# Linear attention and a squared-ReLU layer on one core: the carried product in 64x64 tiles read from the compact state, and a new order of all operations

## Chip, cores and metric

The kernel runs on one core of a Trainium2 chip. The time is device microseconds of one execution; three runs of the kernel before took 183.14, 184.62 and 185.03 us. The engines are TensorE (PE in the profile, with its weight loads as PEld), VectorE (DVE), ScalarE (ACT), GpSimd (POOL) and SyncE (SP), whose queue issues all DMAs here.

## The reference

```python
def _attn_ref(r, k, v, w, u):           # (4, 8, 768, 48) each, u (8, 48)
    for t in range(S):
        cur = einsum('bhd,bhe->bhde', u[None] * kt, vt)
        y[:, :, t] = einsum('bhd,bhde->bhe', rt, state + cur)
        state = wt[:, :, :, None] * state + einsum('bhd,bhe->bhde', kt, vt)
...
    x = attn_out.transpose(0, 2, 1, 3).reshape(B * S, H * D)     # 3072 x 384
    g = maximum(x @ w_in, 0) ** 2                                # 3072 x 2048
    return g @ w_out                                             # 3072 x 384
```

A linear attention with a decay per channel runs over 768 positions for 4 batches of 8 heads of width 48. Its output is the input of a two-layer network with a squared ReLU between the layers.

## The kernel before, in words

**Tiling.** The 768 positions of a batch are cut into three steps of 256 positions, so there are 12 steps s = 0 to 11. Each step has two chunks c = 0, 1 of 128 positions, and a row of a tile holds two neighbouring positions j = 0, 1. The eight heads are treated as four pairs; `e` is the head in a pair. In a chunk, the attention is a masked product within the chunk, and a product of r with the state that is carried over from earlier chunks.

**The operations of a step**, by the names that the order uses (line of the kernel before, engine):

- `ld.s.x` loads w, r, k, v of a step (L168, 384 KB each) on SP; `ld.g.i` and `ld.g.o` load quarters of the two weights (L178, L184), which `cast` makes bf16 (L190, on ACT, DVE or POOL).
- `ww_` multiplies neighbouring decays (L248), `lw_` takes the logarithm (L252, ACT), `cum_` sums it with three kinds of products (L309 to L312, TensorE): two triangular sums and the sum of a chunk. `exp_` (L317) and `ac_` (L322) are exponentials on ACT.
- `rw_`, `kw_` (L273, L277) multiply r and k with decays; `rd_.s.1` and `rd_.s.0` (L335, L332, DVE) make the decayed k and r. They are transposed by TensorE (`tr_`, L346, with copies `rkt_`, L359 and L362) in steps 0 to 3, or by a DMA transpose (`dtr_`, L369, L371) later.
- `p_` (L385, TensorE, 64x64 tiles) makes the scores, `pm_` (L395, L398, DVE) masks them, `y_` (L441) multiplies them with v.
- `ku_`, `qp_`, `q_`, `qs_`, `vq_` (L284, L289, L293, L264, L302) make the term of u and of the position itself; `v_` and `vs_` (L259, L264) are casts of v.
- `su_` (L412, TensorE, 64x64 tiles with 48 columns) makes what a chunk adds to the state, `ts_` (L420, L422) adds it to the state, and `sn_` (L427, POOL) multiplies by the chunk's decay and writes the state S as bf16, 128 rows (two heads of 64) by 4 pairs by 48 columns. This is the compact form.
- `sb_` (L436) copies S into a block-diagonal buffer of 128 rows by 4 pairs by 2 x 48 columns, one copy for each half of the rows, the other half staying zero from four clears at the start (L234, POOL).
- `yc_` (L441 too) is the carried product: for each chunk four products, one for each pair, of full 128x128 weights (r transposed) with 96 columns of that buffer. It adds into the same bank as `y_`.
- `ysb_` (L463, DVE) adds the u term and evicts y, `yt_` and `xt_` (L472, L477) or the DMA transpose `dyt_` transpose it to xT.
- `m1_.s.g` (L492, 8 groups of 6 products), `rl_` (L501 on ACT, L503 on DVE), `sq_` (L509, L511), `m2_.s.c.q` (L517, 8 pieces of 4 products), `os_` (L524, L526) and `store` (L530) are the two-layer network.
- `warm_.n.b` (L534) issues n filler products into bank b; nothing reads them.

**What sets the order.** One string, ORDER, lists every operation. The program records them in that order, and each engine runs its own operations strictly in the order of the list, SP's DMAs too. A suffix `=A`, `=V`, `=G` picks ACT, DVE or POOL, and `:0`, `:1`, `:m`, `:b` pick the PSUM bank. PSUM holds two double banks `att`, two banks `bk` and two banks `m`.

The carried product, its buffer and the list's start:

```python
    def sb_(s, c):
        t = tiles["S", s + c, 1 - c]
        b = tiles["sb", s + c, 1 - c] = sb_bufs[(2 * s + c - s // NB) % NSB]
        for e in range(2):
            rows = slice(e * DP, (e + 1) * DP)
            copy_on("sb_", s, c)(b[rows, :, e, :], t[rows])
...
ld.0.w ww_.0=V ld.0.k kw_.0=G lw_.0 warm_.9.0 cum_.0:0 exp_.0 rd_.0.1 warm_.8.1 tr_.0.1:0 rkt_.0.1=A ld.0.r
```

Of the kernel before, what the change touches and what calls it, by code (L numbers as in the profile page):

```python
# [22 lines left out]
rkt_.1.1=V vs_.1.0=A v_.1=A warm_.1.2 tr_.1.0:1 ysb_.0=V lw_.2 rkt_.1.0=V warm_.4.2 yt_.0:0 sn_.0.1 sb_.0.1=A
ac_.1 vs_.1.1=G q_.1 qs_.1=G p_.1.1:0 p_.1.0:m vq_.1=G cast.i.2=A cast.i.1=A xt_.0=V pm_.1.0 su_.1:b ts_.1.0=V
cum_.2:1 sn_.1.0 pm_.1.1 cast.i.0=G m1_.0.4:0 m1_.0.5:1 sb_.1.0=A y_.1:0 yc_.1 ts_.1.1=V rl_.0.5=V ysb_.1=V
rl_.0.4=A m1_.0.2:1 rl_.0.2=A ld.2.k m1_.0.3:0 ld.2.r kw_.2=G rl_.0.3=A exp_.2 ld.3.i yt_.1:0 sn_.1.1
m1_.0.0:1 m1_.0.1:0 cast.i.3=G ld.2.v ku_.2=V xt_.1=V rl_.0.0=A ac_.2 rl_.0.1=A m1_.1.0:1 qp_.2=G rw_.2=V
# [5 lines left out]
y_.2:1 yc_.2 m2_.0.0.1 rl_.1.7=A sq_.0.3=A m2_.0.1.2 m2_.0.0.2 m2_.0.1.3 m2_.0.0.3 ww_.3=V lw_.3 ld.3.v
os_.0.1=A os_.0.0=A cum_.3:0 ysb_.2=V yt_.2:1 xt_.2=V exp_.3 ac_.3 rl_.1.5=V sq_.1.3=A sq_.1.2=A m2_.1.0.0:0
m1_.2.3:1 ld.4.w vs_.3.0=G kw_.3=V qp_.3=V m1_.2.1:0 m2_.1.0.1 rw_.3=G rl_.2.1=A v_.3=A rl_.2.3=A m2_.1.0.2
m2_.1.0.3 ww_.4=G m1_.2.5:0 rd_.3.1 su_.3:1 ld.4.r ld.4.k q_.3 vs_.3.1=A rd_.3.0 m1_.2.4:1 os_.1.0=A qs_.3=G
ts_.3.0=A sn_.3.0 rl_.2.4=V tr_.3.1:1 lw_.4 kw_.4=G tr_.3.0:0 rw_.4=G rkt_.3.1=A cum_.4:0 exp_.4 rl_.2.5=V
m1_.2.0:1 ld.4.v rl_.2.0=A m1_.2.2:0 m2_.1.1.0:1 rl_.2.2=A m2_.1.1.1 ts_.3.1=V rkt_.3.0=V sn_.3.1 rd_.4.1
ku_.4=G vq_.3=G p_.3.0:m v_.4=A ac_.4 sq_.2.2=A sb_.3.0=A rd_.4.0 pm_.3.0 ld.6.w su_.4:1 p_.3.1:0 m2_.1.1.2
m2_.1.1.3 ld.5.k pm_.3.1 m1_.2.6:0 y_.3:0 yc_.3 qp_.4=G sq_.2.1=A sq_.2.0=A m1_.2.7:1 ld.5.w os_.1.1=V  # L40
m2_.2.0.0:0 ts_.4.0=V dtr_.4.1 dtr_.4.0 sb_.3.1=A rl_.2.6=A sn_.4.0 ld.6.v ld.6.k ld.5.r ww_.5=G ysb_.3=V q_.4
yt_.3:1 m2_.2.0.1 ts_.4.1=V m2_.2.0.2 p_.4.1:0 p_.4.0:1 rl_.2.7=V sq_.2.3=V xt_.3=A m2_.2.1.0:1 vs_.4.1=A
lw_.5 m1_.3.2:0 store.1.0 m1_.3.3:1 qs_.4=G pm_.4.1 sn_.4.1 rl_.3.2=A vs_.4.0=G cum_.5:0 m1_.3.0:0 rl_.3.3=A
vq_.4=G sb_.4.0=V pm_.4.0 ac_.5 ww_.6=G m1_.3.7:1 exp_.5 m2_.2.0.3 sq_.3.1=A y_.4:1 rl_.3.0=V rl_.3.7=A yc_.4
ld.6.r rw_.6=G m1_.3.1:0 ku_.5=G qp_.5=G m1_.3.4:1 ld.7.w store.1.1 os_.2.0=A ku_.6=G m2_.2.1.1 kw_.5=V
rw_.5=V kw_.6=V rl_.3.1=A lw_.6 m1_.3.5:0 ld.5.v ysb_.4=V store.2.0 cum_.6:1 ww_.7=G ld.8.w yt_.4:0 ld.7.k
kw_.7=G rd_.5.1 rd_.5.0 xt_.4=V rl_.3.4=A sq_.3.0=A rl_.3.5=A exp_.6 m1_.3.6:1 v_.6=A m2_.2.1.2 rl_.3.6=V
m2_.3.0.0:0 m1_.4.3:0 v_.5=A m2_.2.1.3 ac_.6 su_.5:0 rd_.6.1 rd_.6.0 rl_.4.3=V dtr_.5.0 su_.6:1 ts_.5.0=V
sq_.3.2=A sb_.4.1=A dtr_.5.1 q_.5 sq_.3.3=A os_.2.1=A vs_.5.0=A lw_.7 dtr_.6.0 qs_.5=A vs_.5.1=A ld.7.v ld.7.r
m1_.4.7:1 m1_.4.5:0 rl_.4.5=V m2_.3.0.1 m2_.3.0.2 m2_.3.0.3 m1_.4.6:0 ts_.6.0=V sn_.6.0 sn_.5.0 sb_.5.0=A  # L50
ts_.6.1=V qp_.6=G vs_.6.0=G p_.5.1:0 p_.5.0:1 rl_.4.7=V m2_.3.1.0:1 m1_.4.0:1 rl_.4.6=V pm_.5.1 dtr_.6.1
sq_.4.3=A os_.3.0=A vq_.5=G m2_.3.1.1 rl_.4.0=V pm_.5.0 vs_.6.1=A cum_.7:0 m2_.3.1.2 m1_.4.1:0 y_.5:1 ac_.7
# [535 lines left out]
```

## Time and profile before

| | us |
|---|---|
| median of three runs | 184.62 |
| the profiled execution, its own time | 184.86 |
| its span | 182.9 |
| TensorE busy | 173.3 |
| DVE busy | 141.3 |
| ACT busy | 131.9 |
| POOL busy | 114.4 |
| first m1_ product starts | 23.70 |

The span runs from the first to the last instruction that the profiler shows; the execution's own time is 2.0 us more. A row of the groups by form reads: line, engine, operation, tiles, shape and count, then busy time and mean ns of one, then the engine's idle time before these instructions and what ended it. A row of the chain of waits in order of time reads: start, length, what; a row of the timeline likewise with the engine first. TensorE's products overlap in the pipe, so the mean of one product in a group row is longer than the spacing of its starts, and the price of a stretch is read from the starts of what follows.

### The profile page before, as it was taken

The numbers are of one execution on the slowest core, as the hardware profiler recorded it, in microseconds if no ns is written. First come the engines' busy times: TensorE is split into PE (matmuls) and PEld (weight loads), VectorE is DVE, ScalarE is ACT, GpSimd is POOL, SyncE is SP. The second block draws the span as 40 slices with busy tenths as digits, with TensorE's granted clock in tenths as the row PEclk, the third lists the DMA queues.
The fourth block names the chain that finished last, engine by engine and source line by source line (L and its number), as shares of the span: only waits on it lengthen the run. The fifth ranks groups of instructions, "written<-read, shape, count | busy, mean of one in ns | idle before, by whom it ended". The sixth has DMA issues, their size and how long they took to land.

```text
span 182.9 us, 5277 instructions
## 1 busy us (share of the span) xinstructions
PE 173.3 (95%) x2150; PEld 124.2 (68%) x2150; DVE 141.3 (77%) x218; ACT 131.9 (72%) x237; POOL 114.4 (63%) x151
## 2 busy tenths in 40 slices
...
GB/s 141 267 268 303 380 287 345 373 286 236 224 271 142 230 291 292 147 159 199 264 203 167 272 191 189 192 193 282 144 109 87 117 47 88 72 61 86 0 128 90
DMA packets 79208, 35.80 MB, mean 196 GB/s; under 512 B 72400, under 2 KB 77648, under 8 KB 79184
## 3 DMA queue, kind: packets, MB, share of 16 engines
...
q8 instruction: 17, 0.28, 0.7%
...
## 4 chain that ended last, share of the span: by engine, by line
PE 69%; DVE 8%; ACT 8%; DMA 7%; issue 5%; POOL 1%; DVEq 0%; ACTq 0%; POOLq 0%
PE m L492 28%; PE bk L517 27%; DMA xT<-y_sb 5%; PE att L441 4%; PE bk L534 3%; ACT gt L501 2%; PE att L385 2%; DMA w_raw<-in_w_dram 2%; DVE rdec_buf L332 2%; ACT att L317 2%; DVE gt L503 1%; ACT v_bf L259 1%; DVE y_sb L463 1%; ACT gt L509 1%; POOL ku L302 1%
## 5 line engine op out<-in xcount | busy, mean ns | idle before, releaser
L492 PE MATMUL m<-xT,wi_sb 128*128 128x256 bf16 x576 | 73.9, 273 | 1.3 <-DMA xT<-y_sb 1.0
L517 PE MATMUL bk<-wo_sb,gt 128*128 128x384 bf16 x384 | 71.8, 326 | 0.0
L492 PEld LDWEIGHTS <-wi_sb 128*128 128x128 bf16 x576 | 55.0, 98 | 14.4 <-DMA xT<-y_sb 1.8
L501 ACT ACTIVATE gt<-m 128x512 f16<-128x512 f32 x60 | 35.4, 595 | 22.9 <-PE m L492 22.1
L517 PEld LDWEIGHTS <-gt 128*128 128x128 bf16 x384 | 36.7, 98 | 19.4 <-ACT gt L509 0.2
L509 ACT ACTIVATE gt<-gt 128x1024 bf16<-128x1024 f16 x37 | 38.4, 1053 | 4.1 <-DVE gt L503 3.8
L503 DVE TENSOR_SCALAR gt<-m 128x512 f16<-128x512 f32 x36 | 24.6, 687 | 10.6 <-PE m L492 10.3
L398 DVE TENSOR_TENSOR pmT<-att,mask 128x1024 bf16<-128x1024 f32 x19 | 22.8, 1216 | 0.1
L284 POOL TENSOR_TENSOR ku<-k_raw,u_bc 128x768 f32<-128x768 f32 x10 | 18.5, 1854 | 5.0 <-DMA k_raw<-in_k_dram 5.0
L302 POOL TENSOR_TENSOR ku<-v_sh,qs 128x768 f32<-128x768 bf16 x11 | 16.3, 1479 | 1.9 <-ACT qs L264 1.4
L289 POOL TENSOR_TENSOR ku<-ku,r_raw 128x768 f32<-128x768 f32 x9 | 16.7, 1850 | 0.2
L427 POOL TENSOR_TENSOR S<-t_state,ac_buf 128x192 bf16<-128x192 f32 x20 | 11.7, 588 | 4.1 <-DVE t_state L420 1.8
L264 POOL COPY qs<-q 64x8 f32<-64x8 f32 x32 | 6.3, 196 | 12.8 <-DVE q L293 11.7
L335 DVE TENSOR_TENSOR kdec_buf<-k_raw,att 128x768 bf16<-128x768 f32 x12 | 11.4, 948 | 3.7 <-ACT att L317 2.5
L332 DVE TENSOR_TENSOR rdec_buf<-r_raw,att 128x384 bf16<-128x384 f32 x24 | 12.2, 548 | 1.3 <-ACT ac_buf L322 1.1
L534 PE MATMUL bk<-warm 128*128 128x512 bf16 x33 | 11.9, 510 | 1.2 <-DVE half_ones L220 1.2
L264 POOL CAST v_sh<-v_raw 64x384 bf16<-64x384 f32 x20 | 10.7, 535 | 3.2 <-DMA v_raw<-in_v_dram 2.3
L463 DVE TENSOR_TENSOR y_sb<-att,ku 128x768 bf16<-128x768 f32 x12 | 11.4, 953 | 1.5 <-PE att L441 0.7
L436 ACT COPY sb_buf<-S 64x192 bf16<-64x192 bf16 x32 | 11.1, 346 | 2.0 <-POOL S L427 1.8
L524 ACT ACTIVATE o_sb<-bk 128x384 f32<-128x384 f32 x12 | 5.8, 487 | 8.7 <-PE bk L517 8.1
L277 POOL TENSOR_TENSOR k_raw<-k_raw,w_raw 128x384 f32<-128x384 f32 x8 | 8.7, 1082 | 5.2 <-DMA k_raw<-in_k_dram 5.2
L511 DVE TENSOR_TENSOR gt<-gt 128x1024 bf16<-128x1024 f16 x11 | 7.8, 715 | 5.3 <-ACT gt L501 5.1
...
## 6 DMA issues: line engine op xcount, KB each, us to landing
...
rT<-rdec_buf SPq DMA_TRANSPOSE x16, 3.5
```

What stands on the lines that cost most here:

```text
L264: copy(out[j * Q:(j + 1) * Q, c], src[c * Q:(c + 1) * Q, :, j])
L284: tensor_mul("ku_", s)(ku[:], raw["k", s][:, :, 1:3, :], u_bc[:, :, None, :].to_broadcast([C, H, 2, D]))
L289: tensor_mul("qp_", s)(ku[:], ku[:], raw["r", s][:, :, 0:2, :])
L302: tensor_mul("vq_", s)(vq[:], tiles["vs", s][:], tiles.pop(("qs", s))[:, :, :, None].to_broadcast([C, 2, H, D]))
L332: nc.vector.tensor_mul(rdec[0][:, :, j, :, 0:D], x[:, :, j, :].rearrange("p (a e) d -> p a e d", e=2), dec.rearrange("p (a e) d -> p a e d ...
L398: nc.vector.tensor_mul(pmT, ps_p[:].rearrange("p e (x t) -> p (e x) t", x=4), mk.to_broadcast([C, 8, C]))
L492: nc.tensor.matmul(ps1[:, j, :], wi_sb[:, n // 4, kk, n % 4 * 128:(n % 4 + 1) * 128], tiles["xT", s][:, :, kk, :], start=(kk == 0), stop=( ...
L501: nc.scalar.activation(rl, m1, AF.Relu, scale=RS)
L503: nc.vector.tensor_scalar(out=rl, in0=m1, scalar1=RS, scalar2=0.0, op0=ALU.mult, op1=ALU.max)
L509: nc.scalar.activation(gt, rl, AF.Square)
L517: nc.tensor.matmul(m2, gt[:, n, c * C:(c + 1) * C], wo_sb[:, n, :], start=(n == 0), stop=(n == NT - 1))
L534: nc.tensor.matmul((bk + m1_bank)[i][:] if i < 4 else att[i - 4][:, 0, :], warm[:, 0:C], warm[:], start=True, stop=True)
```

## The change

- `sb_`, its four buffers and their clears are gone. `yc_` takes a chunk, and makes 16 products for it, one for each pair, position j and head e, of 64x64 weights with 48 columns read from S itself; four of them lie in the four quarters of the array. The list holds 20 such `yc_`, where 12 stood, and places each by itself.
- y lies in its double bank by head e, and no longer by chunk, so `ysb_` reads it in runs of 48. S has six buffers in place of four.
- All operations can take half of the heads, a chunk of a step, or further banks, and there is an operation `al_` that would make the second decay sum on DVE. The list uses no half and no `al_`: both sums stay on TensorE.
- The list is new throughout. By engine, of the operations that changed their place (before, then after): `rw_` POOL 8, 12; `kw_` POOL 8, 10; `ww_` POOL 8, 10; `ku_` POOL 10, 12; `qp_` POOL 9, 11; `qs_` ACT 4, 7; `vs_` DVE 3, 0 and ACT 11, 14; `v_` POOL 4, 2 and ACT 8, 10; `sq_` ACT 37, 41 and DVE 11, 7; `rl_` ACT 60, 59; `os_` ACT 12, 14; casts of the weights on ACT 3, 5, on DVE 2, 0, on POOL 3, 3; `rkt_` ACT 3, 4; filler products 42, 39. TensorE transposes as before in steps 0 to 3, and for y in steps 0 to 5.

```diff
-ld.0.w ww_.0=V ld.0.k kw_.0=G lw_.0 warm_.9.0 cum_.0:0 exp_.0 rd_.0.1 warm_.8.1 tr_.0.1:0 rkt_.0.1=A ld.0.r
-rw_.0=V ld.1.w ww_.1=G rd_.0.0 warm_.4.2 tr_.0.0:1 ld.0.u ku_.0=V qp_.0=V q_.0 ac_.0 lw_.1 ld.1.k ld.0.v
-ld.1.r ld.1.v warm_.1.0 cum_.1:1 rkt_.0.0=A warm_.1.0 p_.0.0:m kw_.1=G ld.2.w pm_.0.0 p_.0.1:0 pm_.0.1 ku_.1=G
...
+ld.0.w ww_.0=V lw_.0 warm_.11.0 cum_.0:0 ld.0.k kw_.0=V exp_.0 rd_.0.1 warm_.8.1 tr_.0.1:0 rkt_.0.1=A ld.0.r
+rw_.0=G rd_.0.0 ld.0.u ld.1.w warm_.3.2 tr_.0.0:1 rkt_.0.0=A ac_.0 ld.0.v ld.1.k ld.1.r ku_.0=G ld.1.v ld.1.i
+warm_.5.2 p_.0.0:1 ww_.1=V qp_.0=V lw_.1 cum_.1:0 ld.0.i v_.0=A su_.0:m ts_.0.0=A pm_.0.0 p_.0.1:1 ld.2.w
+kw_.1=V exp_.1 vs_.0.0=G q_.0 sn_.0.0 vs_.0.1=A rd_.1.1 ld.3.i ld.2.i pm_.0.1 ac_.1 warm_.7.1 tr_.1.1:0
+vs_.1.1=A rkt_.1.1=A rw_.1=G qs_.0=G rd_.1.0 vq_.0=G warm_.2.1 y_.0:1 yc_.0.1:1 tr_.1.0:1 vs_.1.0=A ku_.1=G
+ysb_.0=V ld.2.k cast.i.1=A warm_.1.4 yt_.0:0 rkt_.1.0=V ts_.0.1=V xt_.0=V v_.1=G ld.2.r p_.1.1:0 p_.1.0:m
+pm_.1.0 pm_.1.1 su_.1:b sn_.0.1 yc_.1.0:1 m1_.0.3:0 qp_.1=G cast.i.0=A ld.2.v m1_.0.2:1 rl_.0.3=A ww_.2=G
+warm_.1.4 m1_.0.1:0 q_.1 lw_.2 rl_.0.2=A qs_.1=G ts_.1.0=V sn_.1.0 y_.1:1 warm_.1.4 m1_.0.0:1 cum_.2:0 vq_.1=G
+ld.0.o cast.i.3=A yc_.1.1:1 sq_.0.1=A rl_.0.1=V m1_.0.7:0 ts_.1.1=V rl_.0.0=V cast.i.2=G ld.1.o m1_.0.6:1
+ysb_.1=V rl_.0.7=A yt_.1:0 rl_.0.6=A ld.2.o m1_.0.5:0 exp_.2 rl_.0.5=A sn_.1.1 m1_.0.4:1 xt_.1=V ld.3.o
...
-    NSB = 4
-    sb_bufs = [consts.tile([C, HP, 2, D], BF16, name=f"sb_buf{i}") for i in range(NSB)]
...
-        for t in sb_bufs:
-            nc.gpsimd.memset(t[:], 0.0)
...
-    def sb_(s, c):
...
-    def yc_(s):
-        for c in range(0 if s % NB else 1, 2):
-            for p in range(HP):
-                y_mm(s, c, slice(2 * p * D, (2 * p + 2) * D),
-                     tiles["rT", s][:, c, 2 * p:2 * p + 2, :].rearrange("p j t -> p (j t)"),
-                     tiles["sb", s, c][:, p].rearrange("p e d -> p (e d)"))
+    def yc_(s, c):
+        rT, S_c = tiles["rT", s], tiles["S", s, c]
+        for p in range(HP):
+            for j in range(2):
+                for e in range(2):
+                    y, fresh = y_bank(s, e, slice(j * Q, (j + 1) * Q))
+                    rows = slice(e * DP, (e + 1) * DP)
+                    nc.tensor.matmul(y[:, c, p, :], rT[rows, c, 2 * p + j, :], S_c[rows, p, :],
+                                     start=fresh, stop=True, skip_group_check=True)
...
+        nc.vector.tensor_add(
+            tiles["ysb", s][:, x].rearrange("p c (a e d) -> p (c a) e d", e=2, d=D),
+            tiles["y", s][:, :, cols].rearrange("p e (x d) -> p x e d", d=D),
+            tiles["vq", s][:, x].rearrange("p c (a e) d -> p (c a) e d", e=2))
```

More of the change, by code (lines that the diff above doesn't have):

```diff
@@ L23 @@
[L23 to L27, printed above, removed]
@@ L33 @@
[L33 to L37, printed above, removed]
@@ L38 @@
[L38 to L52, printed above, removed]
@@ new lines @@
+m2_.4.1.0:0 ld.8.r pm_.6.1 exp_.7 rw_.7=G ww_.8=G yt_.5:1 xt_.5=A store.3.0 rd_.7.0 m2_.4.1.1 kw_.7=G sn_.6.1
+ku_.7=G lw_.8 m1_.4.5:0 rl_.4.5=A qs_.6=A m1_.5.0:1 sq_.4.2=A store.2.1 rl_.5.0=V m2_.4.0.0:1 m1_.5.3:0
+vq_.6=G ac_.7 m2_.4.0.1 y_.6:0 dtr_.7.0 rl_.5.3=V rd_.7.1 m1_.5.5:1 qp_.7=G m1_.5.2:0 v_.7=A yc_.6.1:0 su_.7:1
+ysb_.6=V rl_.5.5=A dyt_.6 vs_.7.1=A rl_.5.2=A dtr_.7.1 m1_.5.7:1 m2_.4.0.2 ts_.7.0=V rl_.5.7=A sn_.7.0
+m1_.5.6:0 cum_.8:0 sq_.5.1=A rl_.5.6=V kw_.8=G rw_.8=G exp_.8 m1_.5.4:1 rl_.5.4=A q_.7 m1_.5.1:0 rl_.5.1=V
```

353 lines of the change are left out of this document (200 added, 153 removed).

## The prediction

> **What bounds the kernel now.** I read the table of engines first, then the chain of waits in order of time, then the groups by form, then TensorE's timeline.
>
> ```profile
> PE 173.3 (95%) x2150; PEld 124.2 (68%) x2150; DVE 141.3 (77%) x218; ACT 131.9 (72%) x237; POOL 114.4 (63%) x151
> ```
>
> TensorE is busy 95% of a span of 182.9 us. Whether that is work or waiting is read from the chain, which gives the price of each kind of TensorE work in a dense stretch (start, length, what):
>
> ```profile
> 29.70 1.45 PE m L492 x12
> 31.99 0.89 PE bk L346 x16
> 49.89 0.37 PE att L412 x32
> 58.72 0.59 PE att L441 x20
> 62.25 0.58 PE att L385 x32
> 62.83 0.76 PE bk L517 x4
> 67.28 0.74 PE att L441 x24
> 87.08 0.36 PE att L385 x16
> 127.16 1.31 PE m L492 x12
> 128.47 1.30 PE bk L517 x8
> 174.37 5.21 PE bk L517 x32
> ```
>
> The reader is to see unit prices. A first-layer group m1_ (6 products) costs 1.31/2 = 0.655 us, a second-layer piece m2_ (4) 1.30/2 = 0.65. Transposes cost 0.89/16 = 0.056 each. The rows of 20 and 24 differ by four carried products, so one chunk of yc_ costs 0.15 us and y_ 0.44. From 29.70 on, where the seventh m1_ group starts, TensorE still has 90 m1_ (59.0 us), 96 m2_ (62.4) and the attention of ten steps: y_ and yc_ 10 x 0.74 less three half ones 0.45 (6.95), 9 cum_ at 0.43 (3.9, timeline rows below), p_ and su_ 9.7 (prices below), 4 yt_ and 4 tr_ (56 transposes, 3.1). That is 145.0 us of work. The last product ends at 174.37 + 5.21 = 179.6, so 3.3 us are tail. 182.9 - 29.7 - 145.0 - 3.3 = 4.9 us are stalls. So the kernel is 29.7 us of opening and then TensorE's own work, with little to win between.
>
> ```profile
> 44.17 0.24 PE L309 MATMUL att<-half_ones,lw_buf 128*128 128x2 bf16 x4
> 44.60 0.50 PE L472 MATMUL bk<-ident,y_sb 128*128 128x128 bf16 x6
> ```
>
> **Part 1, the carried product.** The old form is 80 full-array products; the new one is 320 products of 64x64 with 48 columns (20 chunks of 16), the shape of su_ at L412 (64x64, 48 columns). The p_ rows of 16 and 32 give what a run of small tiles costs: the second 16 add 0.58 - 0.36 = 0.22, so 0.14 us is entry; and four m2_ products after a run take 0.76 instead of 0.65, so 0.11 us is exit. A run costs 0.25 us beside its work. su_ then has 0.37 - 0.14 = 0.23 for 32, so 16 cost 0.115, and a chunk of yc_ that stands next to other small tiles is 0.035 us cheaper than today's 0.15, while one that stands alone costs 0.365. In the two orders I count 17 runs of small tiles before and 24 after; from the seventh m1_ group on, 14 and 19. Of the 20 chunks, 17 come after that point. Sum: 5 x 0.25 - 17 x 0.035 = +0.7 us on TensorE. (p_ and su_ above: 14 x 0.25 + 10 x 0.67 less four half su_ 0.46 = 9.7.) Bounds: 0 if all hides behind stalls; if the small products ran at p_'s 0.22 us per 16, 17 x 0.07 + 1.25 = +2.4. I take 0.7, from the same shape.
>
> [...]
>
> **Part 2, the copies of the state go.** sb_ leaves ACT and DVE, four clears leave POOL, and yc_ waits for sn_ directly, so the state is there two copies (2 x 0.346 = 0.7 us) earlier. Where it is late all the same, whatever stands behind that yc_ in TensorE's list waits with it. The eviction ysb_ now reads its bank in runs of 48; L463 takes 0.953 and two L332 pieces of 384, which read so, 1.10, so it costs DVE 0 to 12 x 0.14 = 1.8 us, off the path. I take 0.
>
> ```profile
> L436 ACT COPY sb_buf<-S 64x192 bf16<-64x192 bf16 x32 | 11.1, 346 | 2.0 <-POOL S L427 1.8
> L436 DVE COPY sb_buf<-S 64x192 bf16<-64x192 bf16 x8 | 2.3, 290 | 0.1
> L264 DVE CAST v_sh<-v_raw 64x384 bf16<-64x384 f32 x6 | 3.4, 564 | 0.1
> L284 POOL TENSOR_TENSOR ku<-k_raw,u_bc 128x768 f32<-128x768 f32 x10 | 18.5, 1854 | 5.0 <-DMA k_raw<-in_k_dram 5.0
> L289 POOL TENSOR_TENSOR ku<-ku,r_raw 128x768 f32<-128x768 f32 x9 | 16.7, 1850 | 0.2
> L302 POOL TENSOR_TENSOR ku<-v_sh,qs 128x768 f32<-128x768 bf16 x11 | 16.3, 1479 | 1.9 <-ACT qs L264 1.4
> L427 POOL TENSOR_TENSOR S<-t_state,ac_buf 128x192 bf16<-128x192 f32 x20 | 11.7, 588 | 4.1 <-DVE t_state L420 1.8 <-DVE t_state L422 1.0 <-ACT t_state L420 0.8
> L264 POOL COPY qs<-q 64x8 f32<-64x8 f32 x32 | 6.3, 196 | 12.8 <-DVE q L293 11.7
> L273 POOL TENSOR_TENSOR r_raw<-r_raw,w_raw 128x384 f32<-128x384 f32 x8 | 8.0, 999 | 1.9 <-DMA r_raw<-in_r_dram 1.8
> ```
>
> **Part 3, the new order's split.** POOL gains two ku_ and two qp_ (4 x 1.85 = 7.4 us), four rw_, two kw_, two ww_ (8 x 1.0 = 8.0), and loses 12 of the small qs copies (2.4) and a few casts and clears: about +10, to 124. ACT gives up 11.1 of sb_ and takes four squares, casts and qs copies for about as much. DVE sheds at least 2.3 + 3.4 of the rows above and four rw_, four squares, two ku_: some 15 to 20 us. All this lies beside TensorE in part 1's terms, as long as no engine's list becomes longer than TensorE's. Before, DVE and ACT are that full; after, POOL and ACT are. I therefore keep the 4.9 us of stalls (bounds 1.5 and 10, in the rivals).
>
> **Part 4, the opening.** The filler products at the start become 11 instead of 9, ww_.0's load, k's multiply (now DVE) and cum_.0 keep their times.
>
> ```profile
> 1.19 4.02 PE L534 MATMUL bk<-warm 128*128 128x512 bf16 x9 [1.19 <-DVE half_ones L220]
> 5.93 0.26 PE L309 MATMUL att<-half_ones,lw_buf 128*128 128x2 bf16 x4 [0.72 <-ACT lw_buf L252]
> 6.65 3.62 PE L534 MATMUL bk<-warm 128*128 128x512 bf16 x8
> 7.78 0.95 DVE L335 TENSOR_TENSOR kdec_buf<-k_raw,att 128x768 bf16<-128x768 f32 x1 [2.52 <-ACT att L317]
> 10.06 0.76 PE L346 MATMUL bk<-ident,kdec_buf 128*128 128x128 bf16 x8
> 10.65 1.03 PE L534 MATMUL m<-warm 128*128 128x512 bf16 x4
> ```
>
> Eight fillers from 6.65 hold TensorE until 10.06, 0.43 us each; the four at 10.65 take about 0.22 each. The first transposes wait for those slow fillers, since their input is ready at 8.75 (7.78 + 0.95, the row of L335). TensorE came to full speed about 4 us after the 0.72 us gap at 5.2 to 5.9, though it had worked 4.0 us before the gap. Eleven fillers end at about 6.0 and close that gap. I take it that full speed comes by about 7, and the transposes start at 8.9. Bounds: 10.2 (no change, and 0.1 us later through the two more fillers) and 8.8. [...]
>
> ```profile
> L362 ACT COPY kT<-bk 128x1024 bf16<-128x1024 bf16 x2 | 2.0, 1004 | 3.2 <-PE bk L346 3.2
> L252 ACT ACTIVATE lw_buf<-ww 128x384 bf16<-128x384 f32 x12 | 6.2, 519 | 3.0 <-DVE ww L248 2.9
> L259 ACT CAST v_bf<-v_raw 128x768 bf16<-128x768 f32 x8 | 6.5, 832 | 0.0
> L317 ACT ACTIVATE att<-att 128x768 f32<-128x768 f32 x12 | 9.6, 802 | 1.1 <-PE att L312 1.0
> L332 DVE TENSOR_TENSOR rdec_buf<-r_raw,att 128x384 bf16<-128x384 f32 x24 | 12.2, 548 | 1.3 <-ACT ac_buf L322 1.1
> L398 DVE TENSOR_TENSOR pmT<-att,mask 128x1024 bf16<-128x1024 f32 x19 | 22.8, 1216 | 0.1
> L395 DVE TENSOR_TENSOR pmT<-m,mask 128x512 bf16<-128x512 f32 x10 | 6.4, 685 | 2.2 <-PE m L385 2.2
> L463 DVE TENSOR_TENSOR y_sb<-att,ku 128x768 bf16<-128x768 f32 x12 | 11.4, 953 | 1.5 <-PE att L441 0.7 <-issue 0.6 <-POOL ku L289 0.2
> L293 DVE TENSOR_REDUCE q<-ku 128x16 f32<-128x768 f32 x12 | 11.4, 946 | 0.6 <-POOL ku L289 0.5
> L477 DVE COPY xT<-bk 128x768 bf16<-128x768 bf16 x5 | 2.8, 553 | 2.3 <-PE bk L472 2.3
> L190 POOL CAST wi_sb<-w_st 128x1536 bf16<-128x1536 f32 x2 | 2.9, 1464 | 1.1 <-DMA w_st<-in_moe_w_in_dram 1.1
> ```
>
> From 8.9 I walk the new order with these means. ACT: from 9.6 two copies (2.0), ac_ and lw_ (0.7), v_.0 (0.83), su_.0 with its copy (0.7), exp_.1 (0.80) = 14.7. DVE is at q_.0 until 14.95 and then runs without a gap: rd_.1.1 0.95, pm_.0.1 1.22, rd_.1.0 1.10, ysb_.0 0.95, copy 0.7, ts_ 0.35, xt_.0 0.55, pm_.1.0 1.37, pm_.1.1 1.22, q_.1 0.95 = 24.3 (the 0.7 and 0.35 are estimates by size from L477). xt_.0 ends at 20.8 and the first m1_ follows su_.1 and yc_.1.0 at about 21.5. POOL then does qs_ 0.78, sn_ 0.59, vq_ 1.48 and the last cast of the first weights 1.46, so the seventh m1_ starts at 24.3 + 4.3 = 28.6, where before had it at 29.7: -1.1 us, with the same work behind it. Without the early full speed all slides by some 1.2 us and the gain is gone (29.8). The loads: on SP's queue k of step 3 is now the fourth load behind the second weights and not the second. Its first reader waited 5.0 us at L284 before. Now three multiplies (ww_.3, rw_.3, ww_.4, 3.0 us) stand ahead of that reader on POOL, and I price the later landing at 0; bounds 0 to 3.
>
> **The sum.** The profiled execution took 184.86 us, 0.24 over the median of 184.62 and inside 183.14 to 185.03. 184.86 - 1.1 (opening) + 0.7 (carried product) + 0 (stalls, tail: the last pieces keep their sequence of square, m2_, os_ and store) = 184.5 us. Likeliest case's own range: 183.0 to 186.3.
>
> **The rivals.** About 1% (1.85 us) is what can be told from no change.
> *TensorE stays slow at the start:* the seventh m1_ at 29.8: 184.5 + 1.2 = 185.7. For it: one gap is thin evidence.
> *DVE's relief pays:* the chain before runs over DVE's rd_, rl_ and ysb_ at several places; with 15 to 20 us less on DVE, stalls fall from 4.9 to about 1.5: 184.5 - 3.4 = 181.1. Against: ACT stays as full.
> *POOL becomes the bound (slower):* summed over the order from the first m1_ to y_.10, POOL has 113 us of work and TensorE 117. By 28.6 some 5 and 6 us of these are done. POOL's 108 then end at 136.6, TensorE's 111 at 139.6, so the old 4.9 us of stalls cover 139.6 + 4.9 - 136.6 = 7.9 us of waits on POOL. Its rows above show 5.0, 12.8, 4.1, 1.9, 1.9 us of waits. If 12 us of these remain, TensorE waits 12 - 7.9 = 4.1 us more: 188.6. It decides from 7.9 us on. Against: q, on which the largest hangs, comes from a DVE with more room.
> [...]
>
> **How the numbers follow.** Forecast 0.32, slow start 0.08, DVE's relief 0.28, POOL 0.27, 25 ns 0.05. Faster by over 1% (below 182.8): 0.28. Within 1%: 0.32 + 0.08 = 0.40. Slower (above 186.5): 0.27 + 0.05 = 0.32. The range, 181.0 to 189.0, takes in the relief at 181.1 and POOL's 188.6, and leaves out about 2 in 10, the tails beyond them.
>
> **What would show it.** Right: 16 yc_ products in about 0.12 to 0.37 us by their neighbours; fillers at 0.22 us from about 7 on and the first transposes near 8.9; first m1_ near 21.5, seventh near 28.6; POOL above 65% with TensorE's stalls still near 5 us. Wrong: POOL's waits for q or loads followed by TensorE waiting for rd_ or y_sb; a first transpose after 10; a yc_ chunk above 0.4 us.

## The result and the profile after

The changed kernel took 186.62 us (median; 185.55 to 188.41) against 184.22 for the kernel before on the same chip: ratio 1.0104, interval 1.0054 to 1.0153. It is slower by about 2 us, where 184.5 and a small gain were forecast.

The profiled execution of the changed kernel had a disturbed clock (0.83 of full speed from 100 to 110 us, against 1.00 elsewhere), so after 29 us, unless the text says otherwise, the rows come from e2, a copy with one word of the list moved at about 95 us (below; 186.49 us, clock 1.00 throughout).

The engines of the changed kernel:

```profile
PE 172.6 (92%) x2387; PEld 123.6 (66%) x2387; DVE 122.7 (66%) x183; ACT 136.3 (73%) x233; POOL 120.4 (65%) x145
```

DVE lost 18.6 us, POOL gained 6.0 and ACT 4.4. TensorE's share fell from 95% to 92%: what was added is waiting. Its opening (timeline: start, length, engine, what):

```profile
1.19 4.00 PE L577 MATMUL bk<-warm 128*128 128x512 bf16 x11 [1.19 <-DVE half_ones L227]
5.78 0.25 PE L323 MATMUL att<-half_ones,lw_buf 128*128 128x2 bf16 x4 [0.59 <-ACT lw_buf L267]
6.21 1.89 PE L577 MATMUL bk<-warm 128*128 128x512 bf16 x8
8.25 0.62 PE L373 MATMUL bk<-ident,kdec_buf 128*128 128x128 bf16 x8
21.56 1.48 PE L535 MATMUL m<-xT,wi_sb 128*128 128x256 bf16 x12
29.03 2.98 PE L535 MATMUL m<-xT,wi_sb 128*128 128x256 bf16 x24 [0.31 <-ACT gt L544]
```

The fillers run at 0.24 us each from 6.2 on, the first transposes start at 8.25 (10.06 before), the first m1_ at 21.56. Eleven fillers took 4.00 us where nine took 4.02 (0.36 us each against 0.45), so some of them ran near the 0.24 us of the later ones already, and a gap of 0.59 us was still left behind them. e2 starts the seventh m1_ group at 28.43, 1.25 us ahead of before. The carried product in e2's chain of waits:

```profile
68.18 0.37 PE att L492 x32
68.55 0.76 PE bk L560 x4
85.30 0.12 PE att L492 x16
93.97 0.24 PE att L492 x16
```

A chunk of 16 costs 0.12 us beside other small tiles and 0.24 by itself, two cost 0.37, and the full-array work after a run takes the 0.11 us more. So neither the opening nor the product went against the forecast. Where the time went is read from two stretches, up to the seventh m1_ and from there to the end (length, then busy time of TensorE as the first engine). The kernel before, then e2:

```profile
29.68:182.90 153.22, 147.28 (x1838) 109.43 (x1837) 117.90 (x179) 110.89 (x197) 93.27 (x113) 1.00 0.84 180
```

```profile
28.43:184.70 156.27, 147.25 (x2042) 109.11 (x2042) 101.55 (x148) 116.17 (x203) 100.46 (x108) 1.00 0.81 179
```

TensorE is as busy as before (147.3 us), but idle for 9.0 us and not 5.9; 3.3 us of both lie in the tail after 145 us. The stretch is 3.05 us longer, and that less the lead of 1.25 is the span's growth of 1.8. By stages, before and e2:

```profile
30.00:50.00 20.00, 19.90 (x246) 14.99 (x246) 17.82 (x28) 18.08 (x32) 11.98 (x13) 1.00 1.02 290
50.00:84.00 34.00, 32.56 (x490) 24.36 (x479) 28.79 (x46) 30.68 (x60) 29.15 (x35) 1.00 1.10 220
84.00:104.00 20.00, 19.39 (x296) 14.83 (x294) 18.18 (x28) 16.19 (x33) 18.01 (x23) 1.00 1.16 215
104.00:145.00 41.00, 40.54 (x540) 30.48 (x536) 34.80 (x53) 29.57 (x49) 31.86 (x39) 1.00 0.94 177
```

```profile
30.00:50.00 20.00, 18.38 (x232) 13.37 (x231) 14.28 (x22) 15.49 (x22) 16.94 (x19) 1.00 1.06 297
50.00:84.00 34.00, 33.89 (x536) 25.61 (x536) 28.45 (x44) 30.97 (x58) 30.48 (x33) 1.00 0.97 195
84.00:104.00 20.00, 17.67 (x299) 13.40 (x298) 13.67 (x22) 17.72 (x36) 16.86 (x18) 1.00 1.05 226
104.00:145.00 41.00, 39.36 (x629) 29.36 (x629) 29.78 (x41) 31.93 (x59) 32.67 (x37) 1.00 1.04 201
```

Idle in the four stages: 0.10, 1.44, 0.61 and 0.46 us before; 1.62, 0.11, 2.33 and 1.64 in e2. The new list waits from 30 to 50 us, from 84 to 104 and later, and saves 1.3 us between. What these waits are (e2, timelines of ACT and TensorE):

```profile
41.07 1.47 ACT L199 CAST wo_sb<-w_st 128x1536 bf16<-128x1536 f32 x1 [0.85 <-DMA w_st<-in_moe_w_out_dram]
49.42 0.18 ACT L345 ACTIVATE ac_buf<-att 128x8 f32<-128x8 f32 x1 [1.74 <-DVE rdec_buf L357]
```

```profile
42.59 2.85 PE L560 MATMUL bk<-wo_sb,gt 128*128 128x384 bf16 x16 [0.31 <-ACT wo_sb L199]
50.06 0.25 PE L323 MATMUL att<-half_ones,lw_buf 128*128 128x2 bf16 x4 [1.25 <-ACT lw_buf L267]
103.26 0.65 PE L419 MATMUL att<-rT,kT 64*64 64x128 bf16 x32 [1.74 <-DMA kT<-kdec_buf]
```

At 41 us ACT waits for the last quarter of the second weights, and m2_ waits for the cast. At 50 us the sum of step 4 waits for its logarithm, which stands behind `ac_.3`. At 103 us the scores of step 7 wait for a transpose, and at 84.87 they wait 0.60 us for another.

### The profile page after: what moved, and what is told of

The parts are those of the page before. It is cut to its first block, busy times and chain, and to the rows that moved or that the text cites. A ratio compares the mean times of both kernels' runs of the same rounds, so it can differ in the third digit from the quotient of the medians.

```text
span 186.6 us, 5700 instructions
## 1 busy us (share of the span) xinstructions
PE 172.6 (92%) x2387; PEld 123.6 (66%) x2387; DVE 122.7 (66%) x183; ACT 136.3 (73%) x233; POOL 120.4 (65%) x145
## 2 busy tenths in 40 slices
DMA packets 79208, 35.81 MB, mean 192 GB/s; under 512 B 72400, under 2 KB 77648, under 8 KB 79184
## 4 chain that ended last, share of the span: by engine, by line
PE 54%; DMA 4%; DVE 4%; POOL 3%; SPq 3%; ACT 2%; issue 2%; ACTq 0%; POOLq 0%; DVEq 0%
PE bk L560 23%; PE m L535 22%; SPq L400 3%; DMA kT<-kdec_buf 2%; DMA xT<-y_sb 2%; PE att L482 2%; PE att L419 2%; PE att L492 1%; DVE rdec_buf L357 1%; POOL ku L296 1%; POOL ku L315 1%; PE att L325 1%; DVE pmT L430 1%; PE att L445 1%; DVE pmT L433 1%
## 5 line engine op out<-in xcount | busy, mean ns | idle before, releaser
L552 ACT ACTIVATE gt<-gt 128x1024 bf16<-128x1024 f16 x41 | 42.5, 1055 | 1.0 <-DVE gt L546 0.6
L296 POOL TENSOR_TENSOR ku<-k_raw,u_bc 128x768 f32<-128x768 f32 x12 | 21.9, 1825 | 0.3 <-DMA u_bc<-in_u_dram 0.3
L301 POOL TENSOR_TENSOR ku<-ku,r_raw 128x768 f32<-128x768 f32 x11 | 20.0, 1821 | 0.2
L460 POOL TENSOR_TENSOR S<-t_state,ac_buf 128x192 bf16<-128x192 f32 x20 | 10.3, 514 | 12.6 <-DVE t_state L455 10.8
L276 ACT CAST v_sh<-v_raw 64x384 bf16<-64x384 f32 x28 | 14.2, 508 | 4.8 <-PE att L482 3.8
L285 POOL TENSOR_TENSOR r_raw<-r_raw,w_raw 128x384 f32<-128x384 f32 x12 | 12.1, 1005 | 5.4 <-DMA r_raw<-in_r_dram 5.3
L306 DVE TENSOR_REDUCE q<-ku 128x16 f32<-128x768 f32 x12 | 11.3, 946 | 1.9 <-POOL ku L301 1.8
L263 POOL TENSOR_TENSOR ww<-w_raw 128x384 f32<-128x384 f32 x10 | 10.4, 1042 | 3.0 <-DMA w_raw<-in_w_dram 3.0
L569 DVE TENSOR_SCALAR o_sb<-bk 128x384 f32<-128x384 f32 x10 | 5.5, 555 | 9.0 <-PE bk L560 9.0
L339 ACT ACTIVATE att<-att 128x768 f32<-128x768 f32 x12 | 9.6, 801 | 2.4 <-PE att L327 2.4
```

What stands on the lines that cost most here:

```text
L276: copy(out[j * Q:(j + 1) * Q, c], src[c * Q:(c + 1) * Q, :, j])
L285: tensor_mul("rw_", s, h)(raw["r", s][:, hs, 2, :], raw["r", s][:, hs, 1, :], raw["w", s][:, hs, 0, :])
L296: tensor_mul("ku_", s, h)(tiles["ku", s][:, hs], raw["k", s][:, hs, 1:3, :], u_bc[:, hs, None, :].to_broadcast([C, n, 2, D]))
L301: tensor_mul("qp_", s, h)(ku, ku, raw["r", s][:, heads(h), 0:2, :])
L552: nc.scalar.activation(gt, rl, AF.Square)
```

## The experiments

Theory A: the new list leaves too little room for DMA: loads and SyncE's queue run in absolute time, take the opening's lead back, and make TensorE wait. Theory B: the list's own order of words does it, whatever the loads do. The rival from the prediction: the small products themselves cost the time. The expectations use more letters: Q and L stand for theory A, O for the list's wait at 50 us (part of B), M for the small products and P for POOL as the bound. All ratios are to the kernel before on the same chip. Edits of the list are shown by the words that move, with a word or two around them, and not by whole lines.

### e1: the changed kernel again

No edit.

> The changed kernel as it is, for an undisturbed profile and a tighter ratio. Theory Q (the new order's DMA list delays loads and transposes, so TensorE's stalls grow from 4.9 to about 7 us): ratio 1.010 to 1.013, span near 184.8, TensorE idle at the same four places (cum_.4, the kT transpose of step 6, xT of step 6, step 9 to 10). Theory M (small tiles cost more than the 0.7 us that I gave them): the same time, but the rows of yc_ cost over 0.4 us a chunk and the idle places vary. Theory P (POOL is the bound): TensorE's idle times end with POOL's work.

Measured: 186.87 us, 1.0109 (1.0070 to 1.0147). The slowdown repeats.

### e2: step 6's transpose ahead of step 7's

```diff
 y_.6:0
-dtr_.7.0
...
 dyt_.6
+dtr_.7.0
```

> One word of the order moved: the transposes of r of step 7 go to the queue behind the transpose of y of step 6. Theory Q: xT of step 6 lands some 2.5 us earlier, TensorE's 2.0 us of idle before the first product of step 6 shrinks to under 0.5, and the time falls by 1 to 2 us against the changed kernel (ratio to before 1.000 to 1.005). Theories M and P: no change beyond 0.3 us.

Measured: 186.49 us, 1.0102 (1.0069 to 1.0134). The changed kernel's own wait near 102 us:

```profile
102.06 1.74 PE L535 MATMUL m<-xT,wi_sb 128*128 128x256 bf16 x12 [1.96 <-DMA xT<-y_sb]
```

It is gone in e2, but the next product that needs a DMA transpose waits 1.74 us at 103.26 (above). Changing places in a late queue moves the wait.

### e3: the changed kernel with nine fillers

```diff
-lw_.0 warm_.11.0 cum_.0:0
+lw_.0 warm_.9.0 cum_.0:0
```

> The changed kernel with 9 filler products at the start in place of 11, so the gap before the first decay sum is open again. My step on the opening: TensorE stays slow until about 10, the first transposes start at 10.1 in place of 8.3, the first m1_ at about 22.7 in place of 21.6, and the time grows by 1.0 to 1.5 us. If the opening is hidden behind loads, the seventh m1_ stays at 29.0 and the time is the same.

Measured: 186.68 us, 1.0110 (1.0061 to 1.0159): the same time without the early start. Its timelines of TensorE and ACT:

```profile
22.41 1.49 PE L535 MATMUL m<-xT,wi_sb 128*128 128x256 bf16 x12
50.13 0.25 PE L323 MATMUL att<-half_ones,lw_buf 128*128 128x2 bf16 x4 [1.25 <-ACT lw_buf L267]
```

```profile
40.62 1.47 ACT L199 CAST wo_sb<-w_st 128x1536 bf16<-128x1536 f32 x1 [0.19 <-DMA w_st<-in_moe_w_out_dram]
```

The first m1_ starts 0.99 us later than in e2 (21.42), yet cum_.4 only 0.07 later. The last weights come at 40.6 here and at 41.1 in e2, so whoever is early waits for them: m2_ starts at 42.66 and 42.59. In these two traces the lead of the opening has ended behind this load. One pair of traces is thin evidence, though: with the same list and the same loads up to there, cum_.4 starts at 50.06 in e2, 49.70 in e15 and 49.30 in e13, and of e3's other executions it is not known whether they started as late (the last section has nine fillers with an early start).

### e4 and e8: the new product in the old order

e4 takes the new operations in the list of before, without `sb_`; e8 then moves the first chunk of the eight two-chunk steps away from the second.

```diff
-y_.4:1 rl_.3.0=V rl_.3.7=A yc_.4
+y_.4:1 rl_.3.0=V rl_.3.7=A yc_.4.0 yc_.4.1
```

```diff
-y_.4:1 rl_.3.0=V rl_.3.7=A yc_.4.0 yc_.4.1
+yc_.4.0:1 y_.4:1 rl_.3.0=V rl_.3.7=A yc_.4.1
```

> The order of before with the new carried product alone: no copies of the state, and each yc_ replaced in place by its one or two chunks of small products. By my prices a run of small tiles of its own costs 0.25 us, 12 of them 3.0 us, and 20 chunks save 0.7: +2.3 us on TensorE, less what the missing copies free on ACT (11 us of work) and DVE (2 us). Theory Q: +0.5 to +2.3 us, ratio 1.003 to 1.012. Theory M: +4 us or more. If the copies' waits were what held before up: faster, ratio below 0.997.

> The kernel with the product alone, and in the eight steps that have two chunks the first chunk moved ahead of y_, so that one more run of small tiles stands alone in each: eight runs more at 0.25 us, +2.0 us against the product alone (ratio to before 1.015 + 0.011 = 1.026) if entering and leaving the small tiles is what costs. If the product alone is slow for another reason (a wait on the state, the eviction's new reading): within 0.6 us of it, ratio 1.013 to 1.018.

Measured: e4 187.7 us, 1.0154 (1.0108 to 1.0200); e8 189.03 us, 1.0250 (1.0210 to 1.0290). Before has 17 runs of small tiles, e4 29, e8 37. By the prices of the prediction e4 should cost 12 x 0.25 less 20 x 0.035, so 2.3 us; the ratio gives 2.8. e8 should cost 8 x 0.25 = 2.0 more; the ratios give 1.8. TensorE's busy time from the seventh m1_ on is 147.28 us before, 149.14 in e4 and 150.36 in e8, so about two thirds of the cost are its own work; the rest is waits. That e8 has the same products as e4 and only more runs shows what this work is: entering and leaving small tiles. The new list, which puts the chunks beside `p_` and `su_`, has 24 runs.

### e5: the full-array product in the new order

```diff
-            for j in range(2):
-                for e in range(2):
...
-                    nc.tensor.matmul(y[:, c, p, :], rT[rows, c, 2 * p + j, :], S_c[rows, p, :],
...
+            e, a = p % 2, p // 2 * 2
+            y, fresh = y_bank(s, e, slice(0, C))
+            nc.tensor.matmul(y[:, c, a:a + 2, :], rT[:, c, 2 * p:2 * p + 2, :].rearrange("p j t -> p (j t)"),
+                             S_c[:, a:a + 2, :].rearrange("p a d -> p (a d)"), start=fresh, stop=True, skip_group_check=True)
```

> The changed kernel with the carried product in the old shape: four full-array products of 96 columns for each chunk, at the same places of the list and after the same waits, reading the compact state as if it were the block-diagonal one; the values of the carried part are therefore not the reference's, and no copies are made. By the prices of the rows (a run of small tiles 0.25 us, 24 runs become 14, a chunk 0.15 in place of 0.115) TensorE has 1.8 us less work. If the small tiles explain what the change lost after 50 us: 1.2 to 2.0 us faster than the changed kernel, ratio to before about 1.000 to 1.004. If the shape costs nothing and the new order alone is slower: ratio stays at 1.009 to 1.012.

Measured: 187.75 us, 1.0187 (1.0147 to 1.0226). The expectation's count of 14 runs was a mistake: the chunks stand between small tiles, so taking them out leaves 22. By the prices it should have come out within 0.2 us of the changed kernel; it is some 1 us slower, and TensorE is busier, not more idle (from the seventh m1_ on; e2 had 147.25):

```profile
28.66:185.70 157.04, 148.01 (x1838) 110.33 (x1838) 101.18 (x148) 115.72 (x202) 100.53 (x108) 1.00 0.84 178
```

So in this order the small products do not cost time; they save 0.8 us of busy time. Why 0.8 and not 0.1 is not settled.

### e6: step 4's logarithm ahead of step 3's exponentials

```diff
+lw_.4
 exp_.3 rd_.3.0 ac_.3
-lw_.4
```

> The changed kernel with one word moved: the logarithm of step 4 stands ahead of the exponential of step 3 on ScalarE, so it no longer waits behind ac_.3, which waits for rd_.3.0. Theory O (the opening's lead is lost at this wait): cum_.4 starts at 48.8 in place of 50.1, TensorE's idle 1.25 us ahead of it goes, and the time falls by 0.8 to 1.3 us against the changed kernel (ratio to before 1.003 to 1.007). Theory L (the loads bound the stretch to 50 us, whatever the list): the wait comes back at the decayed k and r of steps 3 and 4, and the time stays within 0.4 us.

Measured: 185.56 us, 1.0072 (1.0029 to 1.0116). TensorE's rows:

```profile
48.19 0.24 PE L323 MATMUL att<-half_ones,lw_buf 128*128 128x2 bf16 x4
49.37 1.47 PE L535 MATMUL m<-xT,wi_sb 128*128 128x256 bf16 x12 [0.59 <-ACT gt L544]
```

The wait of 1.25 us at 50 us is gone, and 0.59 comes back behind it: this wait was made by the list (theory B has a part here). Of the single moves it is the only one whose ratio fell, by 0.003 or 0.6 us, and the intervals overlap.

### e7: eleven fillers in the kernel before

```diff
-lw_.0 warm_.9.0 cum_.0:0
+lw_.0 warm_.11.0 cum_.0:0
```

> The kernel before with 11 filler products at the start in place of 9. The clock step alone: TensorE at full speed by 6, first transposes at 8.7 in place of 10.06, first m1_ between 22.3 and 23.0 in place of 23.7. If the stretch to 50 us keeps the lead, 0.5 to 1.3 us faster (ratio 0.993 to 0.997). If loads bound it: ratio 0.999 to 1.002, and step 3's decay sum starts at 44.1 as before.

Measured: 184.59 us, 1.0018 (0.9979 to 1.0056).

```profile
22.34 1.48 PE L492 MATMUL m<-xT,wi_sb 128*128 128x256 bf16 x12
94.02 0.81 PE L517 MATMUL bk<-wo_sb,gt 128*128 128x384 bf16 x4 [0.47 <-DVE o_sb L526]
101.44 1.48 PE L492 MATMUL m<-xT,wi_sb 128*128 128x256 bf16 x12 [0.93 <-DMA xT<-y_sb]
```

The first m1_ is 1.36 us ahead of before (23.70), the product at 101.44 only 0.35 (101.79 before). The lead passes the loads of the weights here and goes later: 0.47 us in a wait for an eviction on DVE that before does not have, and 0.33 in a longer wait for a transpose (0.60 before). An early start is worth nothing that can be told in the old list either.

### e9, e10 and e11: loads in large pieces

e9's edit is shown; e10 and e11 make the same one in the kernel before, e11 with e7's eleven fillers in addition.

```diff
-            in_=src[b, hs, i * T:(i + 1) * T, :].rearrange("h (p j) d -> p h (j d)", j=2))
+            in_=src[b].rearrange("h s d -> (h s d)")[i * T * DM:(i + 1) * T * DM].rearrange("(p h x) -> p h x", p=C, h=H))
```

> The changed kernel, but each load of r, w, k and v reads 3 KB in one piece for each partition instead of eight pieces of 384 B: the same bytes and the same readers, in another arrangement of the rows, so the values are wrong throughout. If the lead that the opening gains is swallowed because the loads and the queue set the pace (theory A), the waits for loads shorten, the state product of step 4 no longer starts as late as 50.06 us, the waits for kT and xT near 84 and 102 us shrink, and the time falls by 2 us or more, to 184.5 or less. If the lead is lost to the list's own order (theory B: lw_.4 behind ac_.3 behind rd_.3.0), cum_.4 still starts near 50 us and the time stays within 1 us of 186.6.

> The kernel before with the same large pieces (values wrong in the same way). Theory A: faster than the kernel before by 1 us or more, since its queue ran near its limit too. Theory B: within 1 us of it (183.7 to 185.7).

> The kernel before with the large pieces and 11 fillers. With small pieces the 1.30 us lead of 11 fillers was held to about 90 us and gone at 102 us, where SyncE's queue and the loads stood. Theory A: with quick loads the lead survives, so this is 1.0 to 1.3 us faster than the same kernel with 9 fillers. Rival (the lead is lost to a wait that the loads have no part in): within 0.4 us of the same kernel with 9 fillers.

Measured: the changed kernel 183.98 us, 1.0001 (0.9960 to 1.0042); before 184.4 us, 0.9982 (0.9940 to 1.0024); before with eleven fillers 184.8 us, 0.9987 (0.9936 to 1.0037). This is the main result. Large pieces take the whole slowdown from the changed kernel, 1.0 to 1.1% or about 2 us, and change nothing that can be told in the kernel before, where theory A had expected a gain of 1 us or more. Not every load became larger, though. The packets under 512 B fell from 72400 in e2 to 47824, by 24 x 1024, so 24 of the 48 loads went in pieces of 3 KB. By the kernel's text these are w and v: the tiles of r and k keep a third slot free in each head, so on the side of the tile their pieces stay at 384 B. The packets of single loads were not counted. e9 from the seventh m1_ on, and two of its stages:

```profile
27.80:181.40 153.60, 146.78 (x2044) 108.99 (x2042) 101.36 (x148) 116.24 (x203) 100.30 (x108) 1.00 0.72 179
30.00:50.00 20.00, 18.75 (x243) 13.77 (x241) 14.28 (x22) 16.32 (x23) 18.88 (x21) 1.00 0.92 286
84.00:104.00 20.00, 20.00 (x330) 15.05 (x320) 15.92 (x23) 18.06 (x36) 17.08 (x17) 1.00 1.03 248
```

```profile
38.96 1.47 ACT L199 CAST wo_sb<-w_st 128x1536 bf16<-128x1536 f32 x1
```

Idle falls from 9.0 to 6.8 us. The cast at 41.07 starts at 38.96 without a wait, and nothing is idle from 84 to 104 us. The first stage keeps 1.25 us, which is again the wait of cum_.4 for its logarithm, now at 48.63; the last keeps its 1.64 (0.88 of it for ACT's gt, 0.76 without a releaser in the trace), as they must if the list makes them. The cast alone proves little: with small pieces it starts at 40.43 in e6 and at 40.62 in e3, after waits of 0.52 and 0.19 us. e11 tells nothing on the lead: e10 with its nine fillers had its first transposes at 7.40 already, e11 at 7.92.

### e13 and e14: large pieces in half of the steps

```diff
+        if s >= 7:
+            rows = src[b].rearrange("h s d -> (h s d)")[i * T * DM:(i + 1) * T * DM].rearrange("(p h x) -> p h x", p=C, h=H)
```

e14 has `s < 7`.

> The changed kernel with the large pieces only in the loads of steps 7 to 11, which are issued from about 65 us on (values wrong in those steps). The changed kernel with small pieces stands at 1.010 of the kernel before, with large pieces everywhere at 1.000. If the price of the loads is paid in the stretch from 83 to 104 us, where POOL waits 1.8 to 2.2 us for step 8's load of w and SyncE's queue issues seven loads ahead of the transposes of step 7, most of the gain remains: 1.000 to 1.004. If it is paid before 60 us, where cum_.4 starts 1.4 us earlier with large pieces: 1.008 to 1.011.

> The counterpart: large pieces only in steps 0 to 6 (values wrong there). Price paid from 83 to 104 us: 1.007 to 1.011. Price paid before 60 us: 1.000 to 1.004. If both stretches carry part of it, this and the late half lie near 1.005.

Measured: late half 184.83 us, 1.0056 (1.0021 to 1.0091); early half 185.56 us, 1.0029 (0.9980 to 1.0078). Both lie between 1.000 and 1.010, which is what a shared price would give, and the stall near 102 us shrinks from 1.96 us to 0.95 in e13 and 1.19 in e14. The shares are not shown: e14's interval takes in the whole gain, and e13's reaches close to none.

### e15: POOL's wait for step 8's load

```diff
-ww_.8=G
 yt_.5:1 xt_.5=A store.3.0 rd_.7.0 m2_.4.1.1 kw_.7=G sn_.6.1 ku_.7=G
+ww_.8=G
```

> The changed kernel with one word moved, the values as in the reference: ww_.8, for whose load POOL waits 1.8 to 2.2 us near 88 us, behind kw_.7, sn_.6.1 and ku_.7, which need no load then. If this wait delays k's decayed rows of step 7, y_sb of step 6 and their transposes, the stall of 1.96 us near 102 us shrinks by a microsecond or more, and the ratio is 1.002 to 1.007. If the transposes are late through SyncE's queue alone, which has stores and loads ahead of them, the stall stays and the ratio is 1.008 to 1.012.

Measured: 186.47 us, 1.0153 (1.0095 to 1.0211).

```profile
91.42 0.81 PE L535 MATMUL m<-xT,wi_sb 128*128 128x256 bf16 x6 [0.89 <-ACT gt L544]
102.46 1.48 PE L535 MATMUL m<-xT,wi_sb 128*128 128x256 bf16 x12 [1.62 <-DMA xT<-y_sb]
```

POOL's wait of 1.79 us at 88 us is gone and the stall at 102 us stays. A wait of 0.89 us at 91.42 is new. So POOL's wait was not what made the stall; the queue is left as the suspect.

### e17: two loads behind the transposes

```diff
 store.2.0 ld.8.w
-ld.9.w
 ld.7.v ld.8.v
-ld.9.r
...
 dtr_.7.1
+ld.9.w ld.9.r
...
-rw_.9=G
...
 ww_.9=G
+rw_.9=G
```

> The changed kernel with two loads of step 9, w and r, moved on SyncE's queue from ahead of the transposes of step 7 to behind them, and rw_.9 behind ww_.9 on POOL (values as in the reference). If the transposes of 95 to 101 us are late because loads stand ahead of them in the queue and use the DMA engines, they are issued 1.5 us or more earlier, the wait of 1.96 us near 102 us falls to 0.5 or less, and the ratio is 1.000 to 1.005. If it is y_sb itself that is late, and not its transpose, the wait stays and the ratio is 1.008 to 1.012. If the two loads are then missed where they are read (ww_.9), a new wait of 1 us or more shows between 104 and 115 us.

Measured: 185.95 us, 1.0139 (1.0104 to 1.0175; the kernel before took 183.53 on this chip, 184.75 to 185.1 on the others). SyncE's queue in the changed kernel and in e17:

```profile
91.07 2.49 SPq L177 DMA_DIRECT2D r_raw<-in_r_dram  x1
93.66 1.84 SPq L573 DMA_DIRECT2D out_dram<-o_sb  x2
95.61 2.55 SPq L400 DMA_TRANSPOSE rT<-rdec_buf  x2
98.25 1.91 SPq L524 DMA_TRANSPOSE xT<-y_sb  x1
```

```profile
87.48 1.28 SPq L177 DMA_DIRECT2D r_raw<-in_r_dram  x1
88.86 1.81 SPq L573 DMA_DIRECT2D out_dram<-o_sb  x2
90.78 3.50 SPq L400 DMA_TRANSPOSE rT<-rdec_buf  x2
94.84 1.21 SPq L524 DMA_TRANSPOSE xT<-y_sb  x1
```

In the changed kernel r's decayed rows are ready at 89.5 us (DVE's 88.46 + 1.01) and their transposes are issued at 95.61, behind loads and stores; xT's stands behind them, issued at 98.25, though its input is ready at 95.2:

```profile
94.22 0.96 DVE L503 TENSOR_TENSOR y_sb<-att,ku 128x768 bf16<-128x768 f32 x1 [1.07 <-PE att L492]
```

Without two of the loads these are issued at 90.78 and 94.84 (y_sb ready at 94.8), and TensorE no longer waits at 102. But the loads that were put off stand ahead of step 8's transposes then:

```profile
112.34 0.65 PE L419 MATMUL att<-rT,kT 64*64 64x128 bf16 x31 [0.35 <-DMA rT<-rdec_buf]
113.66 1.48 PE L535 MATMUL m<-xT,wi_sb 128*128 128x256 bf16 x12 [0.67 <-DMA xT<-y_sb]
```

The queue is shown as the cause at 102 us, and the run as a whole is no faster.

### e12, e16 and e18: words together

e12 is e6 and e2 with step 3's k loaded ahead of its r; e16 is e2, e6 and e15; e18 is e17 and e6.

```diff
+ld.3.k
 ld.3.r
...
-ld.3.k
```

> The changed kernel with three words of its list moved: lw_.4 ahead of exp_.3, dtr_.7.0 behind dyt_.6, and step 3's load of k ahead of its load of r. The first alone gave ratio 1.0072, the second alone 1.0102. If the order of single words is what loses the lead, the three together give 1.000 to 1.006 (184.5 to 185.6 us). If the loads in absolute time take the lead back wherever it is gained, nothing is added to the first word's gain: 1.006 to 1.010.

> The changed kernel with three words moved (values as in the reference): ww_.8 behind ku_.7, lw_.4 ahead of exp_.3 (alone 1.0072), and dtr_.7.0 behind dyt_.6 (alone 1.0102). If the changed kernel's loss is these two places in the list, at 50 and at 102 us, the two stalls go together and the time comes down to that of the kernel before or below: 0.997 to 1.003. If a stall that is taken out at one place comes back at the next load, 1.005 to 1.010.

> The same with lw_.4 ahead of exp_.3 (alone 1.0072) in addition. If the two places add up: 0.996 to 1.002, no slower than the kernel before. If the lead from 50 us is given back at the next wait for a load, it equals the run without this word within 0.3%.

Measured: e12 186.24 us, 1.0108 (1.0049 to 1.0167); e16 186.24 us, 1.0123 (1.0073 to 1.0174); e18 185.44 us, 1.0107 (1.0079 to 1.0135). None adds to what e6 gave alone. Loading step 3's k earlier, the one load that the prediction had named, brought nothing that can be told.

## Why the prediction was wrong, step by step

**The price of the carried product was right in kind.** A chunk took 0.12 to 0.31 us by its neighbours in e2's chain (0.12 to 0.37 forecast), and 12 and 8 more runs cost 2.8 and 1.8 us where 2.3 and 2.0 were worked out. Of the term of +0.7 itself nothing is seen in TensorE's busy time (147.28 before, 147.25 in e2); entries that count as idle may hold it, which was not shown.

**The copies of the state** were off the path, as said. POOL's idle time before S grew from 4.1 to 7.6 us (e2; 12.6 in the changed kernel's profile), and no stall of TensorE ended with it. ysb_ kept its 0.95 us.

**The opening came as forecast, and its -1.1 was not worth anything.** The first transposes started at 8.25 (8.9 forecast), the first m1_ at 21.56 (21.5), the seventh at 29.03, and 28.43 in e2 (28.6). Of the way there, "close that gap" is not what happened: TensorE was fast with 0.59 us of the gap left. That full speed comes by about 7 was the author's estimate, and no run shows that closing the gap brings it: eight fillers took 1.89 us from 6.21 on in the changed kernel, with the gap, and 1.89 from 6.20 on in e2, without it. In the twelve timelines of the opening with eleven fillers the first transposes start between 7.9 and 8.7 us; of the five with nine, two are as early (8.37 and 7.40) and three come at about 10. So part of the lead depends on which execution of the kernel before was profiled. The step that failed is what followed, "so the seventh m1_ starts at 24.3 + 4.3 = 28.6, where before had it at 29.7: -1.1 us, with the same work behind it". Work moves up with the start; the last weights did not (their cast got them at 40.62 us in e3 and 41.07 in e2). In e3 and e2 the lead has ended behind the second weights, in the old list (e7) between 94 and 102 us, by an eviction and a transpose.

**"I price the later landing at 0; bounds 0 to 3" and "I therefore keep the 4.9 us of stalls".** This is the term that was mis-sized. The 4.9 us were too many to begin with: before is idle for 5.94 us from the seventh m1_ on, 3.3 of it in the tail, so its stalls are 2.6 us (5.7 in e2), and the sum of the work had missed 2.3. The stretch from the seventh m1_ grew by 3.05 us; less the 0.7 of the product, stalls grew by 2.35 where 0 was taken. Large pieces (e9) take 9.02 - 6.82 = 2.2 us of idle time away again, and about 2 us by the ratios: that is the price of the loads, as far as larger pieces of w and v show it. It lies inside the bounds, but they were written for step 3's k alone, and no rival or chance was made of them. The idle time that is left, 6.82 us against 5.94 before, is about the product's term more; in it 1.25 us at 50 us and 1.2 from 104 to 145 us are the new list's own, and 0.9 to 1.3 saved between 50 and 84 us too. With 2.2 for the loads, which includes what they take back of the lead, the sum would have been 184.86 - 1.25 + 0.7 + 2.2 = 186.5; e2's profiled execution took 186.49. These figures come from the same traces, so this is a balance and no second proof. The time lies inside the range of 181.0 to 189.0, but by a term that none of the listed rivals covered; that it lies there was luck.

The prediction looked for late loads among POOL's waits in the kernel before, and there they are longer than after: 17.6 us in all against 14.1 in e2, with 4.97 of them at 42.71 for k of step 3. DVE before:

```profile
40.68 0.95 DVE L190 CAST wo_sb<-w_st 128x1536 bf16<-128x1536 f32 x1
```

TensorE was idle for 0.10 us from 30 to 50 us all the same, and DVE made the last cast of the second weights at 40.68 without waiting. The size of a wait does not say what it costs; what stands behind it in the list does. The new list put a cast that gates TensorE at the same moment on ACT, and eleven loads and stores ahead of the transposes that TensorE needs next.

In the changed kernel's rows under e17 SyncE's issues follow each other within 0.11 us, and large pieces gave about 2 us. The kernel before issues the same loads, from 24 to 49 us within 0.13 us of each other too, and large pieces gave it nothing that its interval can tell (0.2%). So how closely the issues follow each other does not say whether anything waits for them.

**The rivals.** TensorE did not start slowly. No run shows the price per small product to which the last chance (0.05) belongs: 16 took 0.12 us beside other small tiles, 7.5 ns each, and 0.24 by themselves, 15 ns each. DVE was relieved by 18.6 us (15 to 20 forecast), and this may have paid a little: before, TensorE waited twice for DVE between 50 and 84 us, and neither wait is left in e2.

```profile
56.23 0.43 PE L385 MATMUL att<-rT,kT 64*64 64x128 bf16 x16 [0.59 <-DVE rdec_buf L332]
75.87 0.44 PE L412 MATMUL att<-v_bf,kdec_buf 64*64 64x48 bf16 x32 [0.85 <-DVE rdec_buf L332]
```

That is the 1.3 us saved in this stage; whether DVE's relief or the new places in the list did it was not tried. POOL did not become the bound: its two largest waits alone (7.6 for the state, 7.8 for r in e2) are over the 7.9 us from which that rival was to decide, yet no stall listed for TensorE after 30 us ends with POOL, and taking out its wait at 88 us did not make the kernel faster. The sum of an engine's waits was no test.

**Open.** No changed list with the reference's values got below the kernel before; the best is e6 (1.0072). How the 2 us are shared among the loads is open too. Whether fewer or earlier loads could be found in another list was not tried.
